# Value projection first in layer 1, later stores of the sequence product, four PSUM banks and ScalarE normalisation in the column product

## Chip, cores and metric

The kernel runs on one core of one Trainium2 chip. The metric is the device time of one execution in microseconds (us): 2414.03 us as the median of three runs (2410.94 to 2416.91). Everything is computed in FP32 accuracy: each operand x is split into a rounded part `hi` and a rest `lo = x - hi`, and a product is three matmuls (hi·hi, hi·lo, lo·hi).

## What is computed

Four layers on x of 2048 rows and 640 columns, attention and Fourier mixing in turn; layers 1 and 3 are attention, 2 and 4 Fourier.

```python
x = x + attention(layernorm(x))     # 32 heads of 20, causal window of 256
x = x + fourier(layernorm(x))
x = x + attention(layernorm(x))
x = x + fourier(layernorm(x))

def fourier(x):                     # two products, real part only
    a = x @ dft_hid_re.T
    b = x @ dft_hid_im.T
    return dft_seq_re @ a - dft_seq_im @ b
```

Attention projects x to q, k and v (`x @ wqkv`), takes a masked softmax of the scores, multiplies by v and projects with `wo`.

## The kernel before

The order on every engine is the order in which the program issues instructions: each engine and the DMA queue of SyncE (SP) work through their own list in order, and a waiting instruction holds all that stand behind it. All transfers are issued on SP. PSUM is one tile of eight banks of 512 columns, and `ROLES` (L41) says which banks each kind of product takes in turn.

**Start of an attention layer (`before_heads`, L259).** x is cut into 16 tiles of 128 rows. `prep` (L283) moves the tiles along: it loads a tile, takes the statistics of tile r+2 (`prep_stats`, VectorE, and the root on GpSimd at L190), normalises tile r+1 (`prep_norm`, L216, in `normalize`, L192, on VectorE) and turns tile r (`prep_turn`, L221): five 128x128 transposes on TensorE, four into a bank of role x4 and one into the bank of role x1, then the `split` (L154) of each into hi (ScalarE) and lo (VectorE). `pieces(sb)` (L305) multiplies two chunks of the q/k weights with the 512 rows of row group sb; it needs four turned tiles. `value(t)` (L313) multiplies tile t with the five splits of the value weights (`load_w`, L237: hi on ScalarE, lo on GpSimd here). In layer 1 nothing is ready; x tiles 0 to 5, interleaved with two q/k chunks, are loaded first, then the value weights; four tiles are turned in the loop at L298, then come pieces(0), values(0), pieces(1). In layer 3 eight tiles are already turned by the layer before, and the order is pieces(0), pieces(1), values(0).

**Heads (`heads`, L451).** Scores, softmax and products with v of 32 heads, with the rest of the projections between them. The change leaves this stage alone.

**Sequence product (`seq`, L998).** Twelve phases in layer order: for each half `sb` of the rows and each `part` (real, imaginary) the phases a, b and g of eight units each (the first a is cut into a1 and a2). One unit loads a 512 KB block of the sequence matrix three units ahead (`load_to`, L923, three buffers `pt`), forms sums and differences of its halves and splits them (`cut_to`, L937, two units ahead; the difference t1 is taken on GpSimd at L947 or L955), and multiplies (L1017): 18 matmuls in a, 15 in b, 21 in g. After the last unit of a phase `gather` (L1041) empties the banks and combines the partial products; its nine stores after g (one after b) to `u_d` are issued on SP at once by `store` (L1053), before the next unit's `load_to`. Four of the nine wait for additions on GpSimd (L1057).

**Column product (`fourier`, from L1189).** `hidden(t)` loads x tile t, multiplies the 128 rows of the sequence product with the hidden matrices in two halves of 30 matmuls (320 columns each, role y, banks 5, 6, 7), adds x on VectorE (L1200) and stores. `load_u` and `cut_u` (L1112, L1119) bring the next 256 rows. In layer 2, from t = 8 on, the tiles for layer 3 are loaded as well, and for t = 12 to 15 two of them are normalised ahead of `hidden(t)` and turned after it; each turned tile's fifth transpose goes to bank 4 (role x1).

Of the kernel before, what the change touches and what calls it, by code (L numbers as in the profile page):

```python
# [7 lines left out]
F32 = mybir.dt.float32  # L8
F32R = mybir.dt.float32r
BF16 = mybir.dt.bfloat16  # L10
AF = mybir.ActivationFunctionType
# [4 lines left out]
P = 128  # L16
# [25 lines left out]
    "t": (0, 1), "s": (2, 3, 4), "pv": (5, 6), "m": (7,), "f": (7, 5, 6), "w": (2, 3, 4, 7),  # L42
    "q": (0, 1), "v": (5, 6, 7), "x4": (2, 3), "x1": (4,),
    "o": (5, 6),
    "y": (5, 6, 7),
}


# [9 lines left out]
class Net:  # L58
    def __init__(self, nc, tc, ctx, a):
        self.nc, self.tc, self.a = nc, tc, a  # L60
        const = ctx.enter_context(tc.tile_pool(name="const", bufs=1))
        self.ln = ctx.enter_context(tc.tile_pool(name="ln", bufs=5))
        self.slots = ctx.enter_context(tc.tile_pool(name="slots", bufs=1))
        psum = ctx.enter_context(tc.tile_pool(name="psum", bufs=1, space=PSUM))
        self.work = ctx.enter_context(tc.tile_pool(name="work", bufs=2))
        dram = ctx.enter_context(tc.tile_pool(name="dram", bufs=1, space=DRAM))

        self.banks = psum.tile([P, 8, 512], F32, name="banks")

        def fixed(name, cols, dt):  # L70
            return const.tile([P, cols], dt, name=name)

        self.ident = fixed("ident", P, F32)
        nc.sync.dma_start(self.ident, a["ident"])
        self.mask = fixed("mask", 384, BF16)
        self.ux = fixed("ux", 384, BF16)
        self.ones = const.tile([1, 128], F32, name="ones")
        nc.vector.memset(self.ones, 1.0)
        self.half = fixed("half", 1, F32)
        nc.vector.memset(self.half, -0.5)  # L80
        self.big, self.home = [None] * 4, [0, 1, 2, 3]
        self.qp, self.kp = [None] * 2, [None] * 2

        self.qk = dram.tile([2, 2 * D, S], F32, name="qk_d")
        self.vd = dram.tile([NQ, P, NB, 96], F32, name="v_d")
        self.ud = dram.tile([2, KC, P, S], F32, name="u_d")
        self.od = dram.tile([H, 32, S], F32, name="o_d")
        self.rd = dram.tile([NSB, H, 512], F32, name="r_d")
        self.xs = [dram.tile([S, D], F32, name=f"x_d{i}") for i in range(3)]
        self.turn = {}  # L90
        self.xn = {}
        self.ready = 0
        self.slot = None
        self.posted = {}
        self.heavy = []
        self.tmp = None
        mask = self.raw()[:, :384]
        nc.sync.dma_start(mask, a["mask"])
        nc.gpsimd.tensor_copy(self.mask, mask)

    def slot_tile(self, name, cols, dt):
        return self.slots.tile([P, cols], dt, name=name, tag=name)
# [89 lines left out]

    def normalize(self, xn, x, st):
        mv, rs = st
        self.nc.vector.tensor_scalar(
            out=xn, in0=x, scalar1=mv[:, 0:1], scalar2=rs[:, 1:2],
            op0=OP.subtract, op1=OP.mult)
# [23 lines left out]
    def prep_turn(self, t):  # L221
        if t >= NB:
            return
        nc = self.nc
        if t % 4 == 0:
            self.take_big(t // 4)
        xn, xnt = self.xn.pop(t)[0], self.xnt(t // 4)
        cs = slice((t % 4) * P, (t % 4 + 1) * P)
        for ks, role in ((range(4), "x4"), (range(4, 5), "x1")):
            p = self.bank(role, P * len(ks))  # L230
            for n, k in enumerate(ks):
                nc.tensor.transpose(p[:, n * P:(n + 1) * P], xn[:, k * P:(k + 1) * P], self.ident)
            k0, k1 = ks[0], ks[-1] + 1
            self.split(xnt[:, 0, k0:k1, cs], xnt[:, 1, k0:k1, cs],
                       p.rearrange("p (k s) -> p k s", s=P))
# [23 lines left out]
    def before_heads(self, xsrc):  # L259
        nc, a = self.nc, self.a  # L260
        self.proj = self.project()
        ready = self.ready
        first = ready == 0
        vst = [t.rearrange("p (q t c) -> p q t c", t=2, c=96) for t in self.pt[:2]]
        for v in self.pt[:2]:
            nc.gpsimd.memset(v, 1.0)
        if first:
            self.take_tmp()
        for t in range(ready, ready + (6 if first else 4)):
            self.prep_load(xsrc, t)  # L270
            if first and t < 2:
                self.load_chunk(t)
        state = [ready, ready + (6 if first else 4)]
        wv = pairs(cuts(self.kp[1], D) + cuts(self.qp[1], D))[:KC]
        spare = (cuts(self.pt[2], D) + cuts(self.pt[3], D) if first else [None] * 4) + [None]
        wl = [self.load_w(wv, a["wv"], [k], at=k, eng=nc.gpsimd, into=spare[k]) for k in range(KC)]
        for f in wl:
            next(f)
        self.prep_stats(ready)
        self.prep_stats(ready + 1)  # L280
        self.prep_norm(ready)

        def prep():  # L283
            r = state[0]
            if state[1] < r + 5:
                self.prep_load(xsrc, state[1])
                state[1] += 1
            self.prep_stats(r + 2)
            self.prep_norm(r + 1)
            self.prep_turn(r)  # L290
            state[0] += 1

        def split_w(n):
            for _ in range(n):
                if wl and next(wl[0], 1) is not None:
                    wl.pop(0)

        while state[0] < 4:  # L298
            if state[0] in (1, 2):
                self.cut_chunk(state[0] - 1)  # L300
            prep()
            if state[0] > 2:
                split_w(2)

        def pieces(sb):  # L305
            for c in range(2):
                for _ in self.piece(c, sb, "q"):
                    pass
                split_w(4)
                if ready or state[0] < 4 * sb + 8:  # L310
                    prep()

        def value(t):  # L313
            v, xt = vst[t // 2 % 2], self.xnt(t // 4)
            rs = slice((t % 4) * P, (t % 4 + 1) * P)
            ps = []
            for hf in range(2):
                p = self.bank("v", 320)
                cs = slice(hf * 320, (hf + 1) * 320)
                self.all3(p, [((xt[:, 0, k, rs], xt[:, 1, k, rs]), (wv[k][0][:, cs], wv[k][1][:, cs]))  # L320
                              for k in range(KC)])
                ps.append(p)
            prep()
            for hf in range(2):
                dst = v[:, 4 * hf:4 * hf + 4, t % 2, 0:84].rearrange("p q (h c) -> p q h c", c=21)[:, :, :, 1:21]
                src = ps[hf].rearrange("p (q h c) -> p q h c", q=4, h=4)
                if hf == 0:
                    nc.scalar.activation(dst, src, AF.Copy)
                else:
                    nc.vector.tensor_copy(dst, src)  # L330
            if t % 2:
                nc.sync.dma_start(self.vd[:, :, t - 1:t + 1, :].rearrange("q p t c -> p q (t c)"),
                                  v.rearrange("p q t c -> p q (t c)"))

        def values(sb):
            for f in wl:
                for _ in f:
                    pass
            for i in range(4):
                value(4 * sb + i)  # L340

        def packed(sb):
            for f in self.pack(0, sb):
                f()

        pieces(0)
        if ready >= 8:
            pieces(1)
            values(0)
        else:  # L350
            values(0)
            pieces(1)
        self.take_qk("kp", 0)
        self.ones_rows(0)
        packed(0)
        packed(1)
        values(1)
        pieces(2)
        self.load_chunk(2)
        packed(2)  # L360
        values(2)
        pieces(3)
        self.cut_chunk(2)
        self.load_chunk(3)
        packed(3)
        values(3)
        self.ones_rows(1)
# [534 lines left out]
    def take_fourier(self):  # L902
# [16 lines left out]
        self.free = deque([0, 1, 2, 3, 4, 7])  # L919
        self.un, self.normed = 0, 0  # L920
        self.acc = {}

    def load_to(self, n):  # L923
        while self.n_load <= min(n, len(self.order) - 1):
# [73 lines left out]
    def seq(self, n):  # L998
        nc = self.nc
        sb, part, ph, j = self.order[n]  # L1000
        self.load_to(n + 3)
        self.cut_to(n + 1)
        self.x_to(n + 1)
        c, x = self.cut_of.pop(n), self.x_of.pop(n)
# [33 lines left out]
        if last:  # L1038
            self.gather(sb, part, ph)

    def gather(self, sb, part, ph):  # L1041

        nc = self.nc
# [7 lines left out]
            self.free.extend(self.acc.pop(name))  # L1051

        def store(k, t, src):  # L1053
            nc.sync.dma_start(self.ud[part, k, :, t0 + t:t0 + t + 512], src)

        def add(eng, out, a, b, op=OP.add):
            eng.tensor_tensor(out=out, in0=a, in1=b, op=op)  # L1057
# [78 lines left out]
    def fourier(self, xsrc, xdst, more):  # L1136
# [32 lines left out]
        for n in range(self.un, total):  # L1169
# [9 lines left out]
            if n == total - 2:  # L1179
# [3 lines left out]
                             [[[qc[0]], [qc[1]]], [[qc[2]], [self.vq[0], self.vq[1], self.rr[0][:, :256]]]]]  # L1183
                self.cut_u(0, 0)
                self.cut_u(0, 1)
        while loads:
            step_w()

        def hidden(t):  # L1189
            x = self.raw()  # L1190
# [12 lines left out]
        for t in range(NB):  # L1203
# [31 lines left out]
            if more and t >= 12:  # L1235
# [4 lines left out]
                if i == 0:  # L1240
                    for k in (6, 7):
                        self.prep_load(xdst, k)
        self.ready = 8


def network(nc, tc, a, layers=4):
# [67 lines left out]
```

## Time and profile before

| | |
|---|---|
| median of three runs | 2414.03 us |
| the profiled execution's own time | 2416.66 us |
| its span in the profile | 2414.9 us |
| start of layer 1 | 0 to 160 us |
| heads of layer 1, with the start of layer 2 | 160 to 700 us |
| sequence product, layer 2 | to 1072 us |
| column product, layer 2 | 1072 to 1225 us |
| start and heads of layer 3, with the start of layer 4 | 1225 to 1900 us |
| sequence product, layer 4 | to 2268 us |
| column product, layer 4 | 2268 to 2413 us |

The engines are written PE (TensorE matmul), PEld (its weight loads), DVE (VectorE), ACT (ScalarE), POOL (GpSimd) and SPq (the queue of SyncE). Rows of the timeline give the start, the time busy, engine, line, operation, output and input, and in brackets the idle time ahead of it and what ended that idle time. Rows of the chain of waits give start, duration and what the end of the program depended on then. A line such as L162 can be that of a helper that many places call.

### The profile page before, as it was taken

The numbers are of one execution on the slowest core, as the hardware profiler recorded it, in microseconds if no ns is written. First come the engines' busy times: TensorE is split into PE (matmuls) and PEld (weight loads), VectorE is DVE, ScalarE is ACT, GpSimd is POOL, SyncE is SP. The second block draws the span as 40 slices with busy tenths as digits, with TensorE's granted clock in tenths as the row PEclk, the third lists the DMA queues.
The fourth block names the chain that finished last, engine by engine and source line by source line (L and its number), as shares of the span: only waits on it lengthen the run. The fifth ranks groups of instructions, "written<-read, shape, count | busy, mean of one in ns | idle before, by whom it ended". The sixth has DMA issues, their size and how long they took to land.

```text
span 2414.9 us, 40687 instructions
## 1 busy us (share of the span) xinstructions
PE 2277.8 (94%) x13584; PEld 1703.6 (71%) x13584; DVE 1579.7 (65%) x3770; ACT 1097.7 (45%) x1853; POOL 1037.6 (43%) x1509
## 2 busy tenths in 40 slices
PE   7999999998899999999999999999888899999999
PEld 6964544455677878789989544445556688787899
DVE  5256676664688879772461667776637888798622
ACT  3125555544555555551121255556445555455410
POOL 4035565755665243330130456657656652242300
PEclk9999999998899999999999999999988999999999
DMA  5545555664434454644536455556644354546543
GB/s 177 180 141 151 167 164 174 186 184 145 155 130 144 147 167 127 216 165 158 170 136 190 142 157 154 172 177 194 187 126 156 129 162 143 172 134 194 185 146 110
DMA packets 219059, 387.13 MB, mean 160 GB/s; under 512 B 39649, under 2 KB 86241, under 8 KB 218849
## 3 DMA queue, kind: packets, MB, share of 16 engines
q1 hardware_dynamic: 218848, 384.53, 50.8%
q8 instruction: 108, 1.77, 0.3%
q14 instruction: 103, 0.84, 0.1%
HBM read 269.48 MB, written 113.77 MB: 159 GB/s over the span
## 4 chain that ended last, share of the span: by engine, by line
PE 65%; POOL 8%; DVE 7%; ACT 7%; DMA 6%; issue 4%; SPq 3%; POOLq 0%; ACTq 0%; DVEq 0%
PE banks L169 30%; PE banks L1017 19%; PE banks L505 7%; PE banks L543 5%; ACT pt L513 4%; PE banks L476 3%; DMA pt<-c 3%; POOL kp L1057 2%; DVE qp L162 1%; POOL big L162 1%; DVE pt L956 1%; POOL pt L947 1%; DVE st L183 1%; POOL pt L519 1%; DMA qp<-qk_d 1%
## 5 line engine op out<-in xcount | busy, mean ns | idle before, releaser
L481 DVE CUSTOM_DVE_ANT_0 ux<-banks,mask 128x384 bf16<-128x384 f32 (+2 forms) x1024 | 544.3, 532 | 244.8 <-PE banks L476 143.4
L513 ACT ACTIVATE pt<-banks 128x768 f32<-128x768 f32 (+2 forms) x512 | 395.0, 771 | 388.8 <-PE banks L505 270.5
L519 POOL TENSOR_SCALAR_AFFINE_SELECT pt<-pt 128x256 f32<-128x256 f32 x512 | 212.9, 416 | 333.7 <-ACT pt L513 326.2
L169 PE MATMUL banks<-big,wc 128*128 128x512 f32 x1200 | 343.6, 417 | 1.2 <-DVE big L162 0.5
L505 PEld LDWEIGHTS banks<-qp,kp 61*128 61x128 f32 x1024 | 101.6, 186 | 272.3 <-ACT pt L513 221.4
L505 PE MATMUL banks<-qp,kp 61*128 61x384 f32 (+2 forms) x1024 | 230.2, 437 | 50.4 <-ACT pt L513 38.1
L169 PEld LDWEIGHTS banks<-big,wc 128*128 128x128 f32 x1200 | 212.2, 191 | 75.1 <-issue 32.1
L162 DVE TENSOR_TENSOR qp<-pt,qp 128x512 fp32r<-128x512 f32 (+1 forms) x226 | 195.9, 886 | 53.1 <-ACT qp L156 51.0
L156 ACT ACTIVATE qp<-pt 128x512 fp32r<-128x512 f32 (+1 forms) x227 | 138.7, 627 | 185.4 <-POOL pt L947 42.1
L543 PE MATMUL banks<-pt,vq 128*32 128x384 f32 (+2 forms) x2816 | 214.3, 402 | 0.0
L476 PE MATMUL banks<-kp,qp 60*128 60x384 f32 (+2 forms) x1024 | 192.9, 344 | 4.8 <-DVE mc L481 4.7
L523 POOL TENSOR_SCALAR_AFFINE_SELECT pt<-pt 128x256 f32<-128x256 f32 x448 | 185.9, 415 | 0.0
L955 POOL TENSOR_TENSOR pt<-pt,pt 128x512 f32<-128x512 f32 x40 | 87.3, 2194 | 224.1 <-ACT c L156 137.6
L1017 PE MATMUL banks<-qp,big 128*128 128x512 f32 x576 | 150.8, 412 | 27.1 <-POOL big L162 9.0
L1200 DVE TENSOR_TENSOR x<-banks,x 128x320 f32<-128x320 f32 x64 | 30.0, 488 | 191.1 <-PE banks L169 105.3
L1017 PEld LDWEIGHTS banks<-qp,big 128*128 128x128 f32 x576 | 112.0, 198 | 58.9 <-POOL big L162 10.9
L156 ACT ACTIVATE c<-pt 128x512 fp32r<-128x512 f32 x184 | 113.6, 626 | 75.5 <-DVE pt L956 38.4
L162 DVE TENSOR_TENSOR c<-pt,c 128x512 fp32r<-128x512 f32 x184 | 143.0, 793 | 2.6 <-ACT c L156 1.4
L476 PEld LDWEIGHTS banks<-kp,qp 60*128 60x128 f32 x1024 | 111.2, 188 | 25.3 <-DVE mc L481 12.0
L1017 PE MATMUL banks<-c,big 128*128 128x512 f32 x468 | 120.0, 402 | 9.5 <-POOL big L162 4.1
L169 PE MATMUL banks<-big,pt 128*128 128x320 f32 x768 | 119.6, 312 | 2.7 <-DVE x L1200 2.7
L1017 PE MATMUL banks<-qp,xc 128*128 128x512 f32 x480 | 117.4, 392 | 4.7 <-DVE xc L162 4.0
(180 smaller groups left out, 4273.0 us busy)
## 6 DMA issues: line engine op xcount, KB each, us to landing
pt<-c SPq DMA_DIRECT2D x188, 512.0 KB
qk_d<-c SPq DMA_DIRECT2D x80, 512.0 KB
kp<-qk_d SPq DMA_DIRECT2D x384, 80.0 KB
qp<-qk_d SPq DMA_DIRECT2D x384, 80.0 KB
kp<-u_d SPq DMA_DIRECT2D x32, 640.0 KB
o_d<-ou SPq DMA_DIRECT2D x64, 256.0 KB
x_d<-x SPq DMA_DIRECT2D x48, 320.0 KB
v_d<-pt SPq DMA_DIRECT2D x16, 768.0 KB
```

The source lines that it names most:

```text
L156: nc.scalar.activation(hi, src, AF.Copy, scale=-1.0 if neg else 1.0)
L162: (eng or nc.vector).tensor_tensor(out=lo, in0=src, in1=hi.bitcast(F32), op=OP.subtract)
L169: self.nc.tensor.matmul(p, x, y, start=n == 0, stop=n == last)
L476: nc.tensor.matmul(p, qp[quad % 2][b:b + 60, z, qb * P:(qb + 1) * P], kp[quad % 2][b:b + 60, z, k0 * P:(qb + 1) * P], start=True, stop=True)
L481: nc.vector.tensor_tensor_reduce(out=self.ux[:, :n * P], in0=p, in1=self.mask[:, 384 - n * P:], scale=1.0, scalar=NEG, op0=OP.add, op1=OP.max,
L505: nc.tensor.matmul(p, kp[quad % 2][b:b + 61, z, kb * P:(kb + 1) * P], qp[quad % 2][b:b + 61, z, kb * P:(kb + n) * P], start=True, stop=True)
L513: nc.scalar.activation(pt[quad, kb][:, 2 * z:2 * z + 2, :n * P], self.banks[:, 0:2, :n * P], AF.Exp, scale=SCALE)
L519: nc.gpsimd.affine_select(out=t[:, :, 0:P], in_=t[:, :, 0:P], pattern=[[0, 2], [1, P]], compare_op=OP.is_ge, fill=0.0, base=0, channel_mul ...
L523: nc.gpsimd.affine_select(out=t[:, :, 256:384], in_=t[:, :, 256:384], pattern=[[0, 2], [-1, P]], compare_op=OP.is_gt, fill=0.0, base=0, ch ...
L543: nc.tensor.matmul(acc[quad, bk][32 * h:32 * h + 32, (qb - 4 * bk) * P:(e - 4 * bk) * P], vq[:, 96 * (kb % 4) + 21 * h:96 * (kb % 4) + 21 ...
L955: nc.gpsimd.tensor_tensor(out=t1, in0=p, in1=t1, op=OP.subtract)
L1017: nc.tensor.matmul(self.banks[:, bk, :], p, b[q], start=start and m == 0, stop=stop and last and m == 2, skip_group_check=True)
```

## The change

Five edits. (1) `memset` of the two v tiles goes from GpSimd to VectorE in layer 1; two x tiles, the value weights, then the other x tiles and the two chunks, then the mask are loaded in this order; two tiles are turned, the value weights split, and four `value(t)` run before `pieces(0)` and `pieces(1)`. (2) `store` in `gather` puts its transfers on a list; `leave` issues three of them in the next phase's second unit and the others in its third, each time behind `load_to`, and all that are left behind the last unit. (3) Role y gets bank 0 as its fourth bank. (4) While `hid` is set (during the column product) the fifth transpose takes banks 4 and 1 in turn. (5) While `hid` is set `normalize` works with a negated mean from GpSimd and two ScalarE passes instead of one on VectorE.

```diff
-    "y": (5, 6, 7),
+    "y": (5, 6, 7, 0), "x1h": (4, 1),
...
-        self.ready = 0
+        self.ready, self.hid = 0, False
...
-        mask = self.raw()[:, :384]
-        nc.sync.dma_start(mask, a["mask"])
-        nc.gpsimd.tensor_copy(self.mask, mask)
...
     def normalize(self, xn, x, st):
         mv, rs = st
+        if self.hid:
+            nm = self.ln.tile([P, 1], F32, name="nm", tag="nm")
+            self.nc.gpsimd.tensor_scalar_mul(nm, mv[:, 0:1], -1.0)
+            self.nc.scalar.activation(xn, x, AF.Identity, bias=nm, scale=1.0)
+            self.nc.scalar.activation(xn, xn, AF.Copy, scale=rs[:, 1:2])
+            return
...
-        for ks, role in ((range(4), "x4"), (range(4, 5), "x1")):
+        for ks, role in ((range(4), "x4"), (range(4, 5), "x1h" if self.hid else "x1")):
...
-            nc.gpsimd.memset(v, 1.0)
+            (nc.vector if first else nc.gpsimd).memset(v, 1.0)
         if first:
             self.take_tmp()
-        for t in range(ready, ready + (6 if first else 4)):
+        for t in range(ready, ready + (2 if first else 4)):
             self.prep_load(xsrc, t)
-            if first and t < 2:
-                self.load_chunk(t)
...
         for f in wl:
             next(f)
+        if first:
+            for t in range(2, 6):
+                self.prep_load(xsrc, t)
+                if t < 4:
+                    self.load_chunk(t - 2)
+            mask = self.raw()[:, :384]
+            nc.sync.dma_start(mask, a["mask"])
...
-        while state[0] < 4:
-            if state[0] in (1, 2):
-                self.cut_chunk(state[0] - 1)
-            prep()
-            if state[0] > 2:
-                split_w(2)
...
-        pieces(0)
-        if ready >= 8:
+        if first:
+            split_w(4)
+            prep()
+            split_w(6)
+            prep()
+            for t in range(4):
+                if t in (1, 2):
+                    self.cut_chunk(t - 1)
+                value(t)
+            nc.gpsimd.tensor_copy(self.mask, mask)
+            pieces(0)
+            pieces(1)
+        else:
+            pieces(0)
             pieces(1)
             values(0)
-        else:
-            values(0)
-            pieces(1)
...
+        self.leaving = []
...
         self.load_to(n + 3)
+        if j == 1:
+            self.leave(3)
+        if j == 2:
+            self.leave()
...
+    def leave(self, n=9):
+        for f in self.leaving[:n]:
+            f()
+        del self.leaving[:n]
...
         def store(k, t, src):
-            nc.sync.dma_start(self.ud[part, k, :, t0 + t:t0 + t + 512], src)
+            self.leaving.append(lambda: nc.sync.dma_start(self.ud[part, k, :, t0 + t:t0 + t + 512], src))
...
+        self.leave()
         while loads:
             step_w()
+
+        self.hid = True
...
-        self.ready = 8
+        self.ready, self.hid = 8, False
```

## The prediction

> **What bounds the kernel now.** I read the page first, then the busy time by stage, then the waits of TensorE, and at each wait the chain that led to it.
>
> ```profile
> span 2414.9 us, 40687 instructions
> ```
>
> ```profile
> 700.00:1072.00 372.00, 362.38 (x1582) 295.68 (x1582) 314.66 (x433) 202.81 (x385) 137.55 (x84) 1.00 0.49 159
> ...
> 1900.00:2268.00 368.00, 361.34 (x1571) 295.13 (x1571) 312.75 (x429) 200.99 (x382) 138.50 (x83) 1.00 0.49 158
> ```
>
> These windows are the two sequence products: after the length stands the busy time of PE, then PEld, DVE, ACT and POOL. PE sets the pace, with 9.6 and 6.7 us idle, and DVE comes next (315 of 372). So an edit is worth the PE idle time that it ends, less what it makes. Where g ends and the next a begins PE waits most (its waits from 770 to 1005 us, then from 1970 to 2190; total, times, longest):
>
> ```profile
> PE banks L1017 <- ACT qp L156: 3.6, 3, 1.4
> PE banks L1017 <- DVE qp L162: 3.0, 5, 0.7
> ```
>
> ```profile
> PE banks L1017 <- DVE qp L162: 2.6, 4, 0.7
> PE banks L1017 <- ACT qp L156: 1.5, 2, 0.8
> ```
>
> 6.6 and 4.1 us, at six boundaries. The chain behind the first:
>
> ```profile
> 758.65 3.53 DMA pt<-c
> ...
> 769.40 3.61 POOL kp L1057 x3
> ...
> 775.92 0.32 SPq L1054
> ...
> 776.29 5.77 DMA pt<-c
> ```
>
> The last store waits on SP for GpSimd's additions, and only behind it goes the load of the fourth a unit (776.29). It lands at 782.06, where PE has run dry.
>
> **Stores behind the loads: 10.6 + 1.6 us.** Two rows tell when the loads could have gone:
>
> ```profile
> 762.34 4.99 POOL L947 TENSOR_TENSOR pt<-pt 128x512 f32<-128x512 f32 x1 [5.47 <-DMA pt<-c]
> ...
> 775.86 1.73 POOL L947 TENSOR_TENSOR pt<-pt 128x512 f32<-128x512 f32 x1
> ```
>
> Each load waits for the buffer of the unit three before. The one at 776.29 needs the first a unit's buffer, the next the second unit's, and this is read last by the subtraction that ends at 767.3. With no store ahead of them both land by about 773, though not much of the rest can move: the additions still hold GpSimd to 775.9, the next subtraction ends at 777.6, and the fourth unit's follows to 779.3. Its splits on ACT and DVE (0.6 and 0.7 us each, three in series on DVE) end near 781, against 781.4, when PE finishes the third unit, and 784 for the third operand. So these waits go, though with a slack of one or two us. The stores wait for nothing new: three are ready at 769.5, six at 775.9, and SP reaches them at about 769 and 778. Behind the six stands the load of the seventh unit; taken up below.
>
> ```profile
> 784.08 4.13 PE L1017 MATMUL banks<-qp,big 128*128 128x512 f32 x17 [0.72 <-DVE qp L162]
> ```
>
> ```profile
> 2180.91 5.76 PE L1017 MATMUL banks<-qp,big 128*128 128x512 f32 x17 [0.72 <-DVE qp L162]
> ```
>
> ```profile
> 2183.00:2187.00 4.00, 4.00 (x14) 3.18 (x13) 4.00 (x6) 1.34 (x3) 0.70 (x1) 0.67 0.52 160
> ```
>
> After one of the six boundaries the same 17 matmuls took 1.6 us more, at a granted clock of 0.67: a wait can cost clock too, and I count this one as saved. The Trainium skill ("TensorE: Matmul & The Clock Gate", section "Part 1: The HAM clock gate (the "warmup" mystery)") says that the array falls to half clock after at least one idle window of about 3.4 us. Here it fell behind two waits of 1.5 us together, so the row and the rule differ; by the rule no clock is won or lost by any edit, and the sum below would be 13.1 instead of 14.7 us.
>
> **Fourth bank for the column product: 2.7 us.**
>
> ```profile
> 1074.85 1.27 DVE L1057 TENSOR_TENSOR kp<-kp,banks 128x512 f32<-128x512 f32 x2
> ...
> 1080.19 0.52 SPq L1191 DMA_DIRECT2D x<-x_d  x1
> ...
> 1087.48 3.79 PE L169 MATMUL banks<-big,pt 128*128 128x320 f32 x24 [1.68 <-DVE x L1200]
> ```
>
> ```profile
> 2283.37 3.78 PE L169 MATMUL banks<-big,pt 128*128 128x320 f32 x24 [1.05 <-DVE x L1200]
> ```
>
> The first x tile is loaded behind the last nine stores, so its sum frees the first bank late and the fourth half waits 1.68 and 1.05 us. `leave` empties the list ahead of that load, so the load stays late; a fourth bank puts the wait off by 4.4 us, more than it lasts. Below: 0 if bank 0 were still full of the sequence product, but DVE's last read of a bank ends at 1076.1 (1074.85), ten us before its turn.
>
> **Second bank for the fifth transpose, ScalarE normalisation: 0.7 us.** PE's waits from 1168 to 1250, then rows of that stretch:
>
> ```profile
> PE banks L232 <- DVE big L162: 5.4, 4, 2.2
> ```
>
> ```profile
> 1186.52 0.85 POOL L190 TENSOR_TENSOR rs<-rs,half 128x1 f32<-128x1 f32 x1 [0.68 <-DVE rs L187]
> ...
> 1192.43 5.27 PE L169 MATMUL banks<-big,pt 128*128 128x320 f32 x24
> ...
> 1192.99 1.26 ACT L1129 ACTIVATE qp<-kp 128x1280 fp32r<-128x1280 f32 x1
> ...
> 1198.42 3.68 PE L169 MATMUL banks<-big,pt 128*128 128x320 f32 x24
> ...
> 1202.83 1.15 PE L232 MATMUL banks<-ident,kp 128*128 128x128 f32 x9
> ...
> 1208.60 0.78 POOL L190 TENSOR_TENSOR rs<-rs,half 128x1 f32<-128x1 f32 x1 [0.74 <-DVE rs L187]
> ```
>
> ```profile
> 1229.41 0.89 DVE L183 BATCH_NORM_STATS2 st<-kp 128x6 f32<-128x320 f32 x2 [1.06 <-DMA kp<-x_d]
> ...
> 1232.53 0.77 PE L232 MATMUL banks<-ident,kp 128*128 128x128 f32 x5 [1.36 <-DVE kp L195]
> ```
>
> ```profile
> L814 ACT ACTIVATE big<-big,rs 128x640 f32<-128x640 f32 x32 | 26.6, 831 | 13.5 <-POOL rs L837 11.8
> ```
>
> Of bank 4 PE waits 5.4 us, once with 1.6 us of slow matmuls behind it (5.27 against 3.68); at 1232.53 it waits 1.4 us for tile 8, loaded behind the last store: 8.4 in all. The second bank ends the 5.4 and the 1.6. But the new `normalize` is no longer hidden. It puts two negated means on POOL (no row; between nothing and the root's 0.8 us each; 0.5 for both, as such a small operation is nearest to a short root) and four ACT passes (0.83 each, 3.3 us) between the second root and the second tile's transposes, with `cut_u`'s and the chunk's hi parts and the turned tiles' splits queued behind them on ACT, and DVE waits for these. First pair: 1187.4 + 0.5 + 3.3 = 1191.2, while PE is there at 1189.6: 1.6 us. In the steady state the last transposes end at 1204.0 and the second root at 1209.4, 5.4 us, plus 3.8 makes 9.2; PE needs 8.8 + 0.55 for 60 matmuls and a tile. But in the second and third pair ACT has 1.26 + 0.7 us more to do in that loop: 1.8 us of wait each. The last pair has neither. The end takes 1.1 + 1.4: the bank wait that goes there only lets PE come earlier to the tile 8 whose load is tied to the last store. 1.6 + 1.8 + 1.8 + 2.5 = 7.7, a gain of 0.7. Bounds: 5.9 if ACT is hidden (8.4 - 2.5), and a loss of 2 if the splits queue longer. The wait of 2.5 us at tile 8 may halve the clock as 2.2 did at 1190: minus 0.8, half of 1.6.
>
> **Opening: -0.1 us.**
>
> ```profile
> 4.23 2.69 POOL L266 MEMSET pt<- 128x1536 f32 x2
> ...
> 7.73 0.89 DVE L183 BATCH_NORM_STATS2 st<-big 128x6 f32<-128x320 f32 x2 [1.51 <-DMA big<-x]
> ...
> 9.88 0.89 DVE L183 BATCH_NORM_STATS2 st<-big 128x6 f32<-128x320 f32 x2 [0.31 <-DMA big<-x]
> ...
> 12.24 1.54 POOL L162 TENSOR_TENSOR wc<-x,wc 128x640 fp32r<-128x640 f32 x1
> ...
> 19.99 5.80 PE L169 MATMUL banks<-big,wc 128*128 128x512 f32 x14 [0.54 <-DVE big L162]
> ...
> 25.63 0.71 PE L232 MATMUL banks<-ident,big 128*128 128x128 f32 x5
> ...
> 28.98 0.88 DVE L162 TENSOR_TENSOR big<-banks,big 128x512 fp32r<-128x512 f32 x2
> ```
>
> ```profile
> 36.07 4.40 PE banks L169 x30
> ...
> 54.91 3.45 PE banks L169 x15
> 58.36 0.55 PE banks L232 x5
> ```
>
> Before, four values, four pieces and twelve turned tiles are done at 58.9. Now tile 2 comes behind five weight loads: 0.79 MB more than before, at 1.08 us for each 0.33 MB (7.73 to 9.88) 2.6 us later, less 0.5 for the mask; 12.0 (11 to 13). GpSimd's root of tile 2 stands ahead of three weight splits: 12.0 + 1.3 + 0.8 + 3 x 1.57 = 18.8; from there 18 matmuls at the slow rate of 19.99 (0.41 us for 512 columns, so 0.26 for 320) or warm (0.147) end value(0) at 21.4 to 23.5, 1 either way with the landing; 22.6, in the middle, since matmuls were slow until about 5 us after they came in a row (19.99). The rest: 3 x 4.40 + 4 x 3.45 + 10 x 0.55 = 32.5. New is a wait in front of pieces(1), which needs tile 7 straight from its transposes: the like split ended 4.1 us after its transposes began (25.63, 28.98), of which PE fills about 1, so 3.1 us, and half of 1.6 for the clock. 22.6 + 32.5 + 3.1 + 0.8 = 59.0, 0.1 later; 56 to 62 with the ends. The memset on DVE (1.4 us each as on POOL, up to 2.1) ends by 5.3 and lies under the wait for tile 2. The mask's cast and load move to where POOL and SP have time.
>
> **Sum.** 10.6 + 1.6 + 2.7 + 0.7 - 0.8 - 0.1 = 14.7 us. The profiled execution took 2416.7 us, its span and 1.8 us; it becomes 2402.0. The median of the runs is 2.6 lower: 2414.0 - 14.7 = 2399.3.
>
> **Rivals.**
> (a) ScalarE's passes stay hidden: 5.2 us more, 2394. For: ACT is busy under half of the stage; against: the loop above.
> (b) Another wait follows at the g/a boundary: GpSimd's additions delay the fourth unit's subtraction, and a row of 4.99 us for one subtraction shows how long it can be. Then the 12.2 stay, 2412. Against: one to two us of slack even so.
> (c) Slower: the six stores go out at once, ahead of the seventh unit's load (about 780). 1.57 MB at the mean 160 GB/s is 9.8 us on top of 3.53, landing near 793.5, while it must land by about 790 to be cut for PE at 795: a wait of 3.5 us, and 1.6 for the clock as after 1190. Six boundaries of 5.1 are 31, against the 14.7: 2430. The load at 776.29, behind the same nine stores drawn out over 7 us, paid 2.2 on top; waits begin at about 6, and from about 8 the whole is slower.
> (d) The order doesn't change, since the stores wait anyway: excluded by the chain, and counted to (b).
>
> **How the numbers follow.** Forecast 0.6 (own range 2393 to 2406), (a) 0.15, (b) with (d) 0.18, (c) 0.07. This kernel's measurement tells 0.3%, 7.2 us, from no change: the forecast and (a) lie beyond it, (b) within, (c) beyond it on the other side; so faster 0.75, same 0.18, slower 0.07. The range 2390 to 2411 takes in (a) and half of (b).
>
> **What would show it.** SP: the load that stood at 776.29 issued at about 767, and no PE wait above 0.5 us in the fourth a unit; this failing sinks the forecast. The waits on L1200 gone; those of L232 on bank 4 replaced by waits on ACT L19x, 1.5 to 2 us each; tile 8's wait near 2.5. A wait of about 3 us on DVE's split between 43 and 50 us. A wait on `DMA pt<-c` in units five to seven would speak for (c).

## The result, and the profile after

The changed kernel takes 2404.4 us (median of five runs, 2398.98 to 2407.78), the kernel before beside it 2416.24 us (five runs, 2410.94 to 2419.95): a ratio of 0.9951, with a 95% interval of 0.9932 to 0.9971. That is 11.8 us less, where 14.7 were predicted. The profiled execution is the slowest of the five.

Page of the profile of the changed kernel: span, busy times, and the shares of the chain that ended last.

```profile
span 2406.1 us, 40713 instructions
...
PE 2274.1 (95%) x13584; PEld 1706.2 (71%) x13584; DVE 1576.4 (66%) x3764; ACT 1108.6 (46%) x1869; POOL 1020.8 (42%) x1515
...
PE 70%; POOL 6%; ACT 6%; DVE 6%; DMA 5%; issue 4%; SPq 3%; ACTq 0%; POOLq 0%; DVEq 0%
```

PE now carries 70% of the chain instead of 65%, POOL 6% instead of 8%.

For all kernels the span was cut at the same instructions: the first matmul of the scores of layer 1 and of layer 3, the end of PE's wait for DVE's split of xc at the start of each sequence product, and the first matmul of each column product. "Column, layer 2" runs to the scores of layer 3, so the start of layer 3 is in it. All times are us, one profiled execution each.

| | start | heads 1 | sequence 2 | column 2 | heads 3 | sequence 4 | column 4 | end |
|---|---|---|---|---|---|---|---|---|
| before | 127.5 | 603.0 | 342.0 | 259.0 | 596.6 | 340.9 | 142.3 | 2411.2 |
| after | 129.2 | 600.1 | 333.5 | 259.9 | 605.3 | 333.3 | 141.0 | 2402.4 |
| after, once more | 131.4 | 605.7 | 333.3 | 257.1 | 600.3 | 333.4 | 141.0 | 2402.1 |

The two heads stages, which no edit touches, took 1199.6 us before and 1205.4 and 1206.0 after; over the eleven profiles of this table and the next they lie between 1193.7 and 1206.0. Without them the change is worth 1.8 - 8.5 + 0.9 - 7.6 - 1.3 = -14.7 us in the first profile and 3.9 - 8.7 - 1.9 - 7.5 - 1.3 = -15.5 in the second. That the first equals the predicted sum is chance, as the parts show.

**Sequence product.** Windows over the two stages, first of the kernel before, then of the changed one; after the length stands the busy time of PE, PEld, DVE, ACT and POOL, then the granted clock, the DMA share and GB/s.

```profile
730.44:1072.44 342.00, 334.61 (x1463) 273.88 (x1463) 288.00 (x399) 185.32 (x343) 121.82 (x66) 1.00 0.50 160
1928.04:2268.96 340.92, 336.05 (x1462) 275.10 (x1463) 288.85 (x399) 185.12 (x343) 123.63 (x66) 0.99 0.50 161
```

```profile
729.37:1062.86 333.49, 332.10 (x1462) 274.35 (x1463) 289.54 (x399) 184.74 (x343) 112.64 (x66) 1.00 0.50 164
1928.06:2261.41 333.35, 332.43 (x1463) 274.36 (x1463) 288.13 (x399) 184.65 (x343) 117.14 (x66) 1.00 0.50 164
```

PE's idle time in the stage falls from 7.4 to 1.4 us and from 4.9 to 0.9. The view of PE's waits is empty from 745 to 1005 us and from 1945 to 2200. One wait that is at no boundary, near the end of the stage in layer 2, grew from 0.54 to 1.12 us. SP's own list around the first boundary of the changed kernel shows why; the row below it is the same list from 762 us on:

```profile
756.43 9.04 SPq L945 DMA_DIRECT2D pt<-c  x4
766.37 1.31 SPq L1074 DMA_DIRECT2D u_d<-x  x3
775.47 0.33 SPq L945 DMA_DIRECT2D pt<-c  x1
775.84 4.13 SPq L1074 DMA_DIRECT2D u_d<-kp  x6
780.08 4.58 SPq L945 DMA_DIRECT2D pt<-c  x3
```

```profile
762.21 3.25 SPq L945 DMA_DIRECT2D pt<-c  x2
```

The load that stood at 776.29 is the third of the four, issued at 762.21, five us earlier than the 767 of the prediction; the fourth is the next unit's. The three stores follow at 766.4, and the six, from 775.8, hold up no load that is needed soon.

**Column product of layer 2.** PE's waits from 1160 to 1250 us of the changed kernel, then the chain to the longest one on ScalarE:

```profile
PE banks L235 <- ACT kp L196: 4.3, 4, 2.2
PE banks L235 <- DVE kp L198: 2.7, 1, 2.7
```

```profile
1193.69 0.80 DVE x L1223 x2
1194.49 1.59 DVE big L159 x4
1196.08 0.80 DVE st L180 x2
...
1198.74 0.55 POOL rs L187
1199.29 0.21 POOL nm L194
...
1199.53 0.84 ACT kp L195
...
1201.12 0.82 ACT kp L195
...
1201.97 0.84 ACT kp L196
...
1202.85 1.33 PE banks L235 x5
```

The statistics of the third pair stand on DVE behind `hidden`'s addition and the splits of the pair before. Then the second root, the negated means and four ACT passes of 0.83 us follow in series, 4.1 us from 1198.74. PE waits 2.18 for the first tile and 0.71 for the second.

**Opening.** PE of the changed kernel where `pieces(0)` passes into `pieces(1)`, and the chain behind a later wait, that for tile 14:

```profile
45.48 0.50 PE L166 MATMUL banks<-big,wc 128*128 128x512 f32 x1 [0.63 <-ACT big L153]
48.06 5.07 PE L166 MATMUL banks<-big,wc 128*128 128x512 f32 x14 [2.09 <-DVE big L159]
...
57.42 1.56 PE L166 MATMUL banks<-kp,big 128*128 128x320 f32 x9
```

```profile
68.29 3.85 DMA kp<-qk_d
...
72.16 0.02 SPq L212
...
72.20 4.05 DMA x<-x
...
76.28 0.90 DVE st L180 x2
```

```profile
78.18 1.12 PE L235 MATMUL banks<-ident,x 128*128 128x128 f32 x5 [1.28 <-DVE x L198]
```

Tile 14's load is issued at 72.20, after `packed`'s transfers (L449), and lands at 76.25. PE comes to the tile at 76.9, and the tile's statistics and normalisation, which follow the load, end only at 78.1.

### The profile page after: what moved, and what is told of

Read it like the earlier page. It is cut to its first block, busy times and chain, and to the rows that moved or that the text cites. A ratio compares the mean times of both kernels' runs of the same rounds, so it can differ in the third digit from the quotient of the medians.

```text
span 2406.1 us, 40713 instructions
## 1 busy us (share of the span) xinstructions
PE 2274.1 (95%) x13584; PEld 1706.2 (71%) x13584; DVE 1576.4 (66%) x3764; ACT 1108.6 (46%) x1869; POOL 1020.8 (42%) x1515
## 4 chain that ended last, share of the span: by engine, by line
PE 70%; POOL 6%; ACT 6%; DVE 6%; DMA 5%; issue 4%; SPq 3%; ACTq 0%; POOLq 0%; DVEq 0%
PE banks L166 28%; PE banks L1032 27%; PE banks L515 7%; PE banks L553 5%; ACT pt L523 4%; PE banks L486 3%; POOL big L159 1%; SPq L449 1%; DMA qp<-qk_d 1%; DMA x<-x_d 1%; DVE qp L159 1%; DVE st L180 1%; POOL kp L159 1%; POOL pt L529 1%; POOL pt L533 1%
## 5 line engine op out<-in xcount | busy, mean ns | idle before, releaser
L966 POOL TENSOR_TENSOR pt<-pt,pt 128x512 f32<-128x512 f32 x40 | 69.6, 1747 | 226.3 <-DMA pt<-c 74.7
L1032 PE MATMUL banks<-qp,big 128*128 128x512 f32 x576 | 144.6, 405 | 16.5 <-POOL big L159 8.5
L159 DVE TENSOR_TENSOR c<-pt,c 128x512 fp32r<-128x512 f32 x184 | 150.5, 833 | 4.8 <-ACT c L153 3.6
L1032 PE MATMUL banks<-c,big 128*128 128x512 f32 x468 | 121.3, 405 | 10.6 <-ACT big L153 5.0
```

Of the source, the lines that this page charges most:

```text
L159: (eng or nc.vector).tensor_tensor(out=lo, in0=src, in1=hi.bitcast(F32), op=OP.subtract)
L966: nc.gpsimd.tensor_tensor(out=t1, in0=p, in1=t1, op=OP.subtract)
L1032: nc.tensor.matmul(self.banks[:, bk, :], p, b[q], start=start and m == 0, stop=stop and last and m == 2, skip_group_check=True)
```

## The experiments

The prediction's forecast has three parts: the load moves ahead of the stores and the boundary waits go (stores_only, stores_at_once); ScalarE's passes show up as new waits (scalar_norm_only, vector_norm); the opening is even (opening_fixed). The last three kernels put the mended parts together. The stages of every run, cut as above:

| | start | heads 1 | sequence 2 | column 2 | heads 3 | sequence 4 | column 4 | end |
|---|---|---|---|---|---|---|---|---|
| stores_only | 128.1 | 593.3 | 333.1 | 257.2 | 600.4 | 333.3 | 142.4 | 2387.8 |
| scalar_norm_only | 127.4 | 602.7 | 339.5 | 261.0 | 600.9 | 342.9 | 142.2 | 2416.5 |
| stores_at_once | 131.9 | 601.0 | 333.5 | 257.4 | 598.2 | 333.4 | 141.0 | 2396.3 |
| vector_norm | 132.1 | 600.2 | 334.3 | 250.3 | 599.9 | 334.5 | 141.0 | 2392.2 |
| opening_fixed | 125.8 | 600.3 | 333.2 | 258.0 | 597.6 | 333.2 | 141.0 | 2389.0 |
| all_fixed | 125.4 | 602.5 | 334.5 | 249.9 | 598.0 | 333.5 | 141.0 | 2384.6 |
| all_fixed2 | 122.3 | 605.2 | 334.2 | 253.3 | 597.9 | 334.5 | 141.0 | 2388.3 |
| all_fixed3 | 122.4 | 601.4 | 333.5 | 248.2 | 598.3 | 332.4 | 141.0 | 2377.2 |

**stores_only**: the kernel before with edit (2) alone.

```diff
+        self.leaving = []
...
         self.load_to(n + 3)
+        if j == 1:
+            self.leave(3)
+        if j == 2:
+            self.leave()
...
-            nc.sync.dma_start(self.ud[part, k, :, t0 + t:t0 + t + 512], src)
+            self.leaving.append(lambda: nc.sync.dma_start(self.ud[part, k, :, t0 + t:t0 + t + 512], src))
...
+        self.leave()
```

> The kernel before with the later stores alone. Theory 1: the whole gain of the sequence product comes from the stores, and it is larger than the PE waits that end (12.2 us with one slow stretch) because every wait also costs about 0.25 us for the matmul behind it: each of the two sequence products shrinks by 7.5 to 8.5 us between its first wait on the xc split and the first matmul of the column product (344.3 to about 336 in layer 2, 343.2 to about 336 in layer 4), and the time falls by 16 us. Theory 2: the waits alone count, and the rest in the changed kernel's trace was the clock of that one execution: 338 and 338.5, time down by 12 us or less. The opening and both column products stay as before, within 0.5 us.

Measured: 2400.21 us, ratio 0.9941 (0.992 to 0.9962) to 2412.57 us. The sequence products take 333.1 and 333.3 us, as in the full change, so edit (2) alone does all that is gained there. The expectation counts from PE's first wait on the xc split, 2.3 us earlier (344.3 and 343.2 us before); counted so, the products take 335.4 and 335.6 us, the 336 of theory 1. The time itself, 9 to 19 us less by the ratio's interval, doesn't tell the two theories apart. The column product of layer 2 was expected to stay within 0.5 us and fell by 1.8; the kernel before lost 1.7 us there at half clock, this execution none. Two of PE's waits in that stage:

```profile
1068.99 1.29 PE L169 MATMUL banks<-big,pt 128*128 128x320 f32 x7 [1.15 <-DVE x L1211]
1174.16 0.33 PE L232 MATMUL banks<-ident,kp 128*128 128x128 f32 x1 [2.34 <-DVE big L162]
```

The wait for the first bank stays (1.15), as it should where the fourth bank is missing, and the column product of layer 4 stays at 142.4 us. So the 1.3 us there belong to the fourth bank.

**stores_at_once**: the changed kernel, with all nine stores right behind one load.

```diff
-        if j == 1:
-            self.leave(3)
-        if j == 2:
-            self.leave()
+        if j == 0:
+            self.leave()
```

> The changed kernel, but all nine stores go out right behind the first load after a boundary, so the loads of the fifth and later units stand behind stores that wait for GpSimd's additions. Theory (what counts is only that the fourth unit's load is free; 1.57 to 2.4 MB of stores do no harm): no PE wait of over 1 us behind a boundary, each sequence product 333.5 to 336.5 us. Rival, the prediction's case (c): stores ahead of a load make it land too late: the fifth to seventh units wait 2 us or more for it at each of the boundaries, 339 us or more, waits in the end on DMA pt<-c.

Measured in one execution (2401.73 us): 333.5 and 333.4 us, and no PE wait in the view from 745 to 1005 us or from 1945 to 2200. SP's list:

```profile
759.00 8.33 SPq L945 DMA_DIRECT2D pt<-c  x3
769.91 1.31 SPq L1072 DMA_DIRECT2D u_d<-x  x3
772.12 5.52 SPq L1072 DMA_DIRECT2D u_d<-kp  x6
777.69 20.02 SPq L945 DMA_DIRECT2D pt<-c  x8
```

Nine stores stand ahead of the next load, a harder case than the prediction's rival (c), and nothing waits. Rival (c) falls. What cost the time before is that the one load had the stores ahead of it; spreading the stores over two units gains nothing more.

**scalar_norm_only**: the kernel before with edit (5) alone (the `if self.hid` branch of `normalize`).

> The kernel before, with only the ScalarE normalisation in the column product (one bank for the fifth transpose, three banks, stores and opening as before). Theory: ScalarE's two passes for each tile are not hidden even here; PE waits on ACT L19x at two or more of the four pairs of tiles, the bank waits (5.4 us before) shrink but the sum of both is at least as large as before, and the column product of layer 2 takes 259 us or more. Rival: the passes are hidden under the bank waits, and the stage is at 257 us or below.

Measured in one execution (2421.91 us): 261.0 us for the column product of layer 2 (259.0 before); 1.7 of the 2.0 us are clock, of which this execution lost 3.4 us in the stage and the kernel before 1.7. PE's waits from 1160 to 1250 us:

```profile
PE banks L238 <- DVE big L162: 6.0, 4, 2.8
PE banks L238 <- DVE kp L201: 1.5, 1, 1.5
PE banks L238 <- ACT kp L199: 0.6, 1, 0.6
```

The bank waits (6.0 instead of 5.4) cover most of the passes. ScalarE's own wait is 0.6 us, at one pair and not at two or more as expected, against 4.3 us in the full change. The passes come to light only when the second bank lets PE arrive earlier: the two edits work against each other.

**vector_norm**: the changed kernel without edit (5): one VectorE instruction instead of the negated mean and two passes.

```diff
-        if self.hid:
-            nm = self.ln.tile([P, 1], F32, name="nm", tag="nm")
-            self.nc.gpsimd.tensor_scalar_mul(nm, mv[:, 0:1], -1.0)
-            self.nc.scalar.activation(xn, x, AF.Identity, bias=nm, scale=1.0)
-            self.nc.scalar.activation(xn, xn, AF.Copy, scale=rs[:, 1:2])
-            return
```

> The changed kernel with normalisation back on VectorE, the four banks and the second transpose bank kept. Theory 1: the ScalarE passes are what TensorE waits for at the transposes; without them these waits (0.69, 0.76, 2.18 and 0.71 us) go, nothing follows in their place but tile 8's wait of 2 to 2.7 us, and the column product of layer 2 up to layer 3's first score falls from 259.9 to about 255 us. Rival: VectorE normalises too late as well, with GpSimd holding it up, and waits of 1 to 2 us stand on it instead: 258 to 260.

Measured: 2396.95 us, ratio 0.9934 (0.9911 to 0.9956). The column product of layer 2 takes 250.3 us, 9.6 less than in the changed kernel's first profile and 6.8 less than in its second. PE's waits from 1160 to 1250 us:

```profile
PE banks L229 <- DVE kp L192: 2.6, 1, 2.6
```

That is below the 255 us expected. The four waits for the two-pass normalisation (4.3 us) are gone with no successor. The rest is mostly clock: none was lost in this stage here, 5.1 us in the changed kernel's first profile and 1.7 in its second.

**after_again**: the changed kernel, unaltered.

> The changed kernel once more, unaltered, to see what varies from execution to execution. Theory: the waits come back within 0.3 us each (0.69, 0.76, 2.18, 0.71 and 2.73 in the column product of layer 2), but the stretches at half clock move, so the column product of layer 2 is between 254 and 260 us and the heads stages between 593 and 606 us. Rival: the half clock belongs to the place: the same stretch near 1202 us at 0.66 and 259 to 260.5 us again.

Measured in one execution: 2407.56 us. The waits return within 0.11 us (0.70, 0.76, 2.17, 0.82, 2.78), the clock doesn't. Windows over the same instructions, the longest ScalarE wait and tile 8, first in the changed kernel's first profile, then here (the granted clock stands third from the end):

```profile
1200.00:1210.00 10.00, 8.02 (x37) 7.68 (x38) 4.09 (x12) 5.09 (x10) 2.32 (x5) 0.66 0.20 68
1222.00:1226.00 4.00, 3.69 (x12) 3.16 (x13) 2.62 (x8) 2.09 (x4) 2.02 (x2) 0.57 1.03 386
```

```profile
1207.50:1217.50 10.00, 7.89 (x46) 7.65 (x47) 4.58 (x13) 5.08 (x10) 2.29 (x5) 0.83 0.21 68
1228.00:1232.00 4.00, 3.48 (x18) 2.97 (x19) 2.98 (x8) 2.13 (x4) 2.24 (x2) 1.00 1.03 391
```

Lost clock is (1 - 0.66) x 10 = 3.4 us and (1 - 0.57) x 4 = 1.7 against 1.7 and nothing: 3.4 us of difference, where the stages differ by 2.8. The rival (clock tied to the place) falls.

**opening_fixed**: the changed kernel, tiles 6 and 7 turned behind the first half of `pieces(0)`, and the x loads put ahead of `packed`'s.

```diff
                 split_w(4)
-                if ready or state[0] < 4 * sb + 8:
+                if first and sb == 0:
+                    if c == 0:
+                        prep()
+                        prep()
+                elif ready or state[0] < 4 * sb + 8:
                     prep()
...
         self.ones_rows(0)
+        while first and state[1] < NB:
+            self.prep_load(xsrc, state[1])
+            state[1] += 1
         packed(0)
```

> The changed kernel with tiles 6 and 7 both turned before the second product of pieces(0), and the last two x tiles loaded ahead of the packing transfers. Theory 1: the two waits that the new opening makes (2.7 us for tile 7's split with 1.6 us of slow matmuls, 1.3 us for tile 14's load behind 24 packing transfers, with 0.8 us after it) go, and the first score matmul comes at about 123 us instead of 129.25 (before: 127.5). Rival: VectorE's work in front of the splits only moves the wait; 127 or later.

Measured: 2394.56 us, ratio 0.9922 (0.9901 to 0.9943); the scores begin at 125.8 us, not at 123. PE:

```profile
40.29 0.71 PE L235 MATMUL banks<-ident,big 128*128 128x128 f32 x5
43.61 1.12 PE L235 MATMUL banks<-ident,big 128*128 128x128 f32 x5 [2.61 <-DVE big L198]
```

The loads ahead of `packed` end the wait for tile 14. But two `prep` in a row only move the other wait: tile 7's transposes are due 0.7 us behind the start of tile 6's, while its normalisation was only issued then.

**all_fixed**: opening_fixed and vector_norm together, and tiles 8 and 9 of layer 3 loaded behind `hidden(14)`, their statistics taken and tile 8 normalised ahead of `hidden(15)`, so that tile 8 is ready. The calls that did this at the start of the attention layer are left to layer 1 alone (not shown below).

```diff
+                if i == 3:
+                    self.prep_stats(8)
+                    self.prep_stats(9)
+                    self.prep_norm(8)
...
-                if i == 0:
-                    for k in (6, 7):
+                if i in (0, 2):
+                    for k in ((6, 7), None, (8, 9))[i]:
                         self.prep_load(xdst, k)
```

> The later stores, four banks and second transpose bank, normalisation on VectorE, the mended opening, and tiles 8 and 9 of layer 3 loaded and normalised one column tile earlier. If the parts add: opening -4.5, sequence products -16, column product of layer 4 -1.3, of layer 2 -9.5 (waits of 1.7, 5.4 and 1.4 and 1.6 for the clock), together -31 us against the kernel before, 2385 us. If the waits only move on, -15 to -20.

Measured: 2389.65 us, ratio 0.99 (0.9879 to 0.9921): 22.9 us, between the two expectations. Tile 8's wait is gone, but the next tile's fifth transpose now waits for bank 4, whose split on ACT stands behind the value weights' splits:

```profile
1217.64 0.33 PE L229 MATMUL banks<-ident,kp 128*128 128x128 f32 x1 [1.42 <-DVE big L159]
```

**all_fixed2**: all_fixed, but in the opening only one tile is turned behind the first half of `pieces(0)` and the other between the halves of `value(2)`, and the fifth transposes of tiles 8 to 11 take banks 4 and 7 in turn.

```diff
+    "x1p": (4, 7),
...
                 ps.append(p)
+                if first and t == 2 and hf == 0:
+                    prep()
             prep()
```

> Parts combined, with two changes to the last version of that kind (2389.7 us): in the opening one extra tile is turned between the two halves of the third value, and one between the two pieces, so that PE no longer waits 2.6 us for tile 7's normalisation; and tiles 8 to 11 take the fifth transpose from banks 4 and 7 in turn, so that the 1.4 us wait in front of tile 9 goes. Theory: start of the scores 123 us (125.4 before), the column product of layer 2 to the scores of layer 3 near 248.5 us (249.9), the rest unchanged: 2386 us, 2 to 4 below the last version. Rival: GpSimd's square root or DVE takes over in the opening, the start stays at 125 or above, and the time stays within 1 us of 2389.7.

Measured: 2389.83 us, ratio 0.9885 (0.9854 to 0.9917); 2386 was expected, and against all_fixed nothing is gained. The opening came out as expected: 122.3 us, with no wait above 0.2 us from 19 us on. The column product didn't, 253.3 us instead of 248.5: tile 11's fifth transpose fills bank 7 just ahead of the first value, which takes the same bank, and its split on DVE stands behind a tile's statistics and normalisation.

```profile
1227.20 2.77 PE L166 MATMUL banks<-kp,big 128*128 128x320 f32 x9 [3.46 <-DVE big L159]
```

**all_fixed3**: banks 4 and 6 instead.

```diff
-    "x1p": (4, 7),
+    "x1p": (4, 6),
```

> The version before it, with banks 4 and 6 instead of 4 and 7 for the fifth transpose of tiles 8 to 11. Theory: PE's new wait of 3.46 us at 1227 us came because the first value of layer 3 takes bank 7, which tile 11's fifth transpose had just filled; bank 6 is the third in turn there, so the wait and the slow matmuls behind it go, the column product of layer 2 to the scores of layer 3 takes 248 to 249.5 us (253.3), and the time falls by 3 to 5 us to about 2386. Rival: the value waits for tile 11's splits themselves, the 3.5 us stay, and the stage is at 252 us or above.

Measured: 2382.58 us (2379.89 to 2385.99), ratio 0.9863 (0.9844 to 0.9882) to 2415.52 us. The stage takes 248.2 us, the same first value follows without a wait, and one wait is left there, for a normalisation that took 1.08 us instead of 0.60 (last section):

```profile
1214.59 0.76 PE L229 MATMUL banks<-ident,kp 128*128 128x128 f32 x5 [0.54 <-DVE kp L192]
...
1219.08 1.56 PE L166 MATMUL banks<-kp,big 128*128 128x320 f32 x9
```

It is 32.9 us below the kernel before, and the fastest of all.

## Why the prediction was nearly right

**Stores behind the loads: the mechanism was right, the term too small.** 10.6 + 1.6 = 12.2 us were predicted, 8.5 + 7.6 = 16.1 measured. The boundary waits went entirely, and no successor came at the boundaries, neither rival (b) nor (c). PE's idle time fell by 10.0 us and the lost clock by 1.7. Most of the rest lies in a cost of each wait that the sum left out: a matmul that stands alone takes longer. In the prediction's row at 784.08 PE had waited 0.72 us, so the single matmul at 782.85 took the 0.50 us to 783.36:

```profile
782.85 0.50 PE L1017 MATMUL banks<-qp,big 128*128 128x512 f32 x1 [1.44 <-ACT qp L156]
```

In a row one takes 0.23 (24 in 5.60 us at 778.57 of the changed kernel). The quoted views count 8 and 6 boundary waits; 14 x 0.27 = 3.8 us, which with 10.0 and 1.7 makes 15.5 of the 16.1. No run varies this cost by itself. The Trainium skill ("TensorE: Matmul & The Clock Gate", section "Step-by-step: what each phase is for") says that an isolated matmul can't hide its drain while one in a stream does; the rows agree in direction, and the 0.27 us are theirs.

**Fourth bank: right.** 2.7 us predicted (1.68 + 1.05). The column product of layer 4 falls by 1.3 us (1.05 and one such 0.27), and no wait on VectorE's addition is left in layer 2. That the share of layer 2 is its 1.68 us is inferred from the wait alone.

**Second bank and ScalarE normalisation: the mechanism was right, the sizes were not.** The waits of bank 4 went and waits on ScalarE took their place, as forecast, so rival (a) falls. Predicted were 1.6, 1.8 and 1.8 for three pairs and 2.5 at tile 8, 7.7 in all; measured were 0.69, 0.76, 2.18 + 0.71 and 2.73, 7.1 in all, so that the errors of the single waits cancelled by chance. The step that failed is the reason for the second and third pair, where "ACT has 1.26 + 0.7 us more to do in that loop": in the third pair ACT had been idle for 6.96 us before its first pass and waited for the negated mean on POOL, which waited for late statistics on DVE. The clock cost was set at 0.8 us; it was 5.1 in one execution and 1.7 in the other, and this, more than the waits, makes the difference. Together the two edits were put at -0.1 us (0.7 - 0.8). With about 1.9 us for the fourth bank taken off, the stage changed by +2.8 and 0.0 us, a loss of 0 to 3. vector_norm shows what edit (5) alone costs beside the second bank: 6.8 to 9.6 us.

**Opening: the step failed.** It was put at a loss of 0.1 us; the start of the scores was 127.4 to 128.1 us in the three profiles with the old opening and 129.2, 131.4, 131.9 and 132.1 in the four with the new one, on average a loss of 3.5 us. Up to 57.4 us the working held: value(0) ended at 21.3 us (22.6 predicted), the wait for tile 7 was 0.63 + 2.09 (3.1 predicted), and four values, four pieces and ten turned tiles, where the sum had counted twelve, ended at 57.42, which with the two tiles that the kernel before had turned by its 58.66 (0.55 each) is 58.5. What the prediction left out stands behind: x tiles are loaded as `prep` goes on, and with two tiles fewer turned the load of tile 14 falls behind the transfers of `packed` on SP. PE waits 1.28 us for it in one execution and 2.23 in the next; the kernels vector_norm and stores_at_once, with the same opening, wait 2.36 and 2.78:

```profile
78.73 1.12 PE L235 MATMUL banks<-ident,x 128*128 128x128 f32 x5 [2.23 <-DVE x L198]
```

The clock takes most of the loss: in all four profiles 1.7 us go at half clock behind the wait for tile 7, where 0.8 was predicted, and in the three that wait over two us for tile 14 another 1.7 behind that (in the second profile of the changed kernel the granted clock is 0.57 from 49 to 53 us and 0.86 from 78 to 90). opening_fixed shows the load of tile 14 as the cause of the second wait, since with the loads moved up the wait is gone; all_fixed2 and all_fixed3, with the wait for tile 7 gone too, begin the scores at 122.3 and 122.4 us. The opening's order was 5 us better than the old one, but for these two places.

So the sum came out near the truth by luck: a term that was 3.9 us too small stood against two others, which together were 4.2 us too good in the first profile and 3.5 in the second. The remaining gap of the medians, 11.8 against 14.7, lies within the interval (0.9932 to 0.9971 of 2416.24 is 7 to 16.4 us). In the profiles 5.8 and 6.4 us were lost in the heads stages. As no edit touches these and other kernels had 1193.7 to 1203.6 us there, they are variation between executions, and most of it is clock. The loss (the time multiplied by one less the granted clock), added up over the heads stages of each trace, is 49.5 us before and 54.6 and 52.9 after. Over the eleven profiles it runs from 42.7 to 54.6, and what the heads take without it lies between 1148.8 and 1153.1 us in all of them. Why the clock falls more often in one execution than in another stays open.

## What to carry to other kernels

On a queue that works in order, put a transfer that waits for computation behind the loads that are due first; here this one change of order was worth 16 us of the two sequence products, and how the stores were spread didn't matter. When transfers or tiles are moved, follow each of them past every later group on the same queue, not only to the point where the counts agree again. A bank, a pass or a split that is hidden under another wait comes to light when that wait is removed: opening_fixed, all_fixed and all_fixed2 each ended one wait and met another close behind it.

## What the runs showed of the hardware that was not expected

**The clock after a wait varies from execution to execution.** Behind waits of 2.2 + 0.7 us the loss was 3.4 us once and 1.7 us once; behind 2.7 us at tile 8 it was 1.7 and nothing; and behind stores_only's 2.34 us nothing (granted clock 1.00):

```profile
1174.00:1178.00 4.00, 3.84 (x27) 3.85 (x28) 3.73 (x12) 2.07 (x3) 0.89 (x2) 1.00 0.76 240
```

The losses are multiples of 1.7 us, which is half of 3.4 us. The Trainium skill (the same page, section "Part 1: The HAM clock gate (the "warmup" mystery)") has a free-running window of about 3.4 us; the multiples agree with that window, but the clock fell without any single idle time of that length.

**A VectorE instruction can wait inside its own time.** In all_fixed3 two normalisations, then the GpSimd instruction beside the first:

```profile
1217.07 1.28 DVE L192 TENSOR_SCALAR kp<-kp,mv,rs 128x640 f32<-128x640 f32 x1
...
1221.34 0.60 DVE L192 TENSOR_SCALAR x<-x,mv,rs 128x640 f32<-128x640 f32 x1
```

```profile
1216.42 1.58 POOL L159 TENSOR_TENSOR qp<-x,qp 128x640 fp32r<-128x640 f32 x1
```

The first ends at 1218.35, 0.35 us after GpSimd's (1218.00); the second runs beside no such instruction and takes 0.60. The same 0.35 us lie between the two ends at 1214.18 and 1214.53 in this run, and twice in all_fixed2 (1218.60 and 1218.95, 1222.41 and 1222.76). The Trainium skill ("SBUF — State Buffer", section "Who interferes with whom") says that the two engines share a pair of ports that one holds for its whole instruction; the rows agree.
